# Blocks of 512 tokens in the later MLP parts, and one group for both halves of a query tile

## The chip, the cores and the metric

The kernel runs on one core of a Trainium2 chip. The metric is device time in microseconds (us) of one execution. Five engines work side by side, each through its own queue of instructions in a fixed order: TensorE (PE, matrix products; PEld is its loading of weights), VectorE (DVE), ScalarE (ACT), GpSimd (POOL) and SyncE (SP, which here issues nearly all DMAs).

## The reference

Linear attention with an exponential feature map is followed by two MLPs. There are 4 batches of 576 tokens, 8 heads of 64, 128 features per sign; then 2304 tokens of 512 go through two MLPs with 2048 hidden values each.

```python
def phi(x):
    proj = np.einsum('bhsd,df->bhsf', x, w_phi)
    proj = proj - np.max(np.abs(proj), axis=-1, keepdims=True)
    return np.concatenate([np.exp(proj), np.exp(-proj)], axis=-1)
q_p, k_p = (phi(q), phi(k))
kv = np.einsum('bhsf,bhsd->bhfd', k_p, v)
z = np.sum(k_p, axis=2)
num = np.einsum('bhsf,bhfd->bhsd', q_p, kv)
den = np.einsum('bhsf,bhf->bhs', q_p, z)[..., None] + 1e-06
x = num / den                                    # to (2304, 512)
h = x @ moe_w_in;  g = where(h > 0, h, exp(min(h, 0)) - 1);  x = g @ moe_w_out
h = x @ moe2_w_in; g = h * cos(h);               out = g @ moe2_w_out
```

## The kernel before

`body` builds a list of tasks. A task is a short run of instructions on one engine, with an estimated cost, a due time, the buffers that it writes and reads, and the tasks that it follows. `plan` (called near the end of `body`) then walks a model of the engines: at each step it takes, for the engine that can start first, the ready task with the earliest due time, gives its buffers places out of the lists that they may use, and so fixes the order of every engine. The costs and the due times (`BEGIN`, `BLOCK_A`, `LEAD`, `PACE` and the others at the head of the file) only set this order; on the chip the engines wait for semaphores.

The attention (`shifted`, `keys`, `sums`, `queries`, `results`) goes by tiles of 128 tokens. Heads are split into an even and an odd set of four ("odd" 0 and 1), each with a PSUM bank of its own. For a tile of keys: projection (line 373), maximum of the absolute values and subtraction on DVE (386, 389), two exponentials per set on ACT (423, 426), the product with the values (431) and, for batch 0 only, the sum over keys by a product with ones (437); for the other batches the sums are added up by POOL or DVE and multiplied by ones once (466). For a tile of queries: projection, maximum and subtraction as above, then per set four turns on PE (517), two exponentials (520), 24 small products against the keys' result (535), and the denominator, its reciprocal and the division (543, 546, 549), which write `xy`, the MLP's input.

The MLPs run in three parts: A, the first MLP's hidden tiles 0 to 7 in 9 blocks of 256 tokens (`NA`), between the attention's instructions; B, its hidden tiles 8 to 15; C, the second MLP's 16 hidden tiles. B and C go in 6 blocks of 384 tokens (`NB`) each. In a block, every value of the input is split into a rounded part and a rest (`high`, `low`, 595), and `step` does one hidden tile: `g1`, 12 matmuls into a bank "h" (636: 4 pieces of the input's width, 3 passes each over high and low parts of weight and input), the activation (655, 658, 661 for the first MLP; 670, 673, 676, 679, 682 for the second), its split into high and low (694), and `g2`, 12 matmuls that accumulate into four output banks "y" (644). `AHEAD` sets how many steps `g2` lags. At a block's end four copies and four DMAs take the outputs away (621), or B adds part A's sums from memory (611). Weights come packed and are unpacked on ACT, DVE and POOL (`convert`, 327 to 356).

SBUF places for these pieces are the "units" u0 to u25 (`unit`), of `NB` columns each; the lists `X_U`, `S_A`, `G_A`, `O_A`, `S_B`, `G_B`, `K_B`, `O_B` say which units inputs, split activations, activations and outputs may use. In part C the outputs have three units (17, 24, 25) and the split activations ten.

A change of the shape that the array holds (128 rows by 128 columns in the MLP, 64 by 128 in projections, 128 by 64 and 128 by 32 in the attention's products) is called a switch below.

## Time and profile before

| | us |
|---|---|
| median of 3 runs (1006.4 to 1008.87) | 1006.4 |
| span of the profiled execution, first to last instruction | 1004.8 |
| PE busy in the span | 986.5 |
| DVE busy | 730.0 |
| ACT busy | 496.3 |
| POOL busy | 241.9 |
| first MLP matmul starts at | 52.4 |
| first matmul of 384 columns starts at about | 396 |
| last copy on ACT starts at | 1001.5 |

The table is read from the page, its busy shares and the list of instructions in order of time. PE's busy time counts a matmul from its start to the modelled end of its pipeline, so short waits inside a group don't show in it; the rate of a group is read from the starts of the groups around it.

### The profile page before, as it was taken

How to read it: one execution, taken by the hardware profiler on the slowest of the kernel's cores; microseconds unless marked ns; L12 is line 12 of the kernel's file. 1: busy time of each engine (PE TensorE's matmuls, PEld its weight loads, DVE VectorE, ACT ScalarE, POOL GpSimd, SP SyncE). 2: the span in 40 equal slices, each digit the busy share in tenths (PEclk: the TensorE clock that was granted, in tenths of full speed). 3: DMA queues.
4: the chain of work that ended last, by engine and by line, in shares of the span. 5: the costliest groups of instructions: out<-in, count | busy, mean ns of one | idle time of the engine just before them, and what ended most of it. 6: DMA issues, size and time to landing. Idle time of an engine off the chain costs nothing.

```text
span 1004.8 us, 21194 instructions
## 1 busy us (share of the span) xinstructions
PE 986.5 (98%) x8404; PEld 943.2 (94%) x8404; DVE 730.0 (73%) x1434; ACT 496.3 (49%) x1192; POOL 241.9 (24%) x274
## 2 busy tenths in 40 slices
PE   9999999999999999999999999999999999999998
PEld 6797888998899999999999999999999999999998
DVE  6999788768677986997354699966666666666664
ACT  6987445545545875775232577532332232323322
POOL 2675303103101772774000276400000000000000
PEclk9999999999999999999999999999999999999999
DMA  6463031022102432441012143000000000000000
GB/s 197 163 201 102 7 107 54 30 78 59 39 13 96 151 124 87 160 158 36 8 32 74 64 137 113 29 33 1 1 32 1 1 33 1 33 1 1 32 1 32
DMA packets 46563, 63.30 MB, mean 63 GB/s; under 512 B 6400, under 2 KB 25472, under 8 KB 46464
## 3 DMA queue, kind: packets, MB, share of 16 engines
q1 hardware_dynamic: 46304, 61.88, 18.7%
q8 instruction: 66, 1.08, 0.5%
q14 instruction: 33, 0.27, 0.1%
q10 hardware_dynamic: 160, 0.07, 0.0%
HBM read 52.49 MB, written 9.44 MB: 62 GB/s over the span
## 4 chain that ended last, share of the span: by engine, by line
PE 81%; DVE 8%; POOL 3%; ACT 3%; issue 3%; DMA 1%; DVEq 0%; POOLq 0%; ACTq 0%
PE h L636 21%; PE y L644 20%; PE a L644 13%; PE a L636 13%; PE a L431 4%; PE a L535 4%; PE a L373 3%; POOL l L342 2%; DVE l L338 2%; POOL l L356 2%; PE a L517 1%; DVE l L334 1%; DVE u L694 1%; DVE u L595 1%; ACT l L327 1%
## 5 line engine op out<-in xcount | busy, mean ns | idle before, releaser
L636 PE MATMUL h<-u,h 128*128 128x256 f32 (+1 forms) x1152 | 254.6, 311 | 3.4 <-DVE u L661 3.4
L644 PE MATMUL y<-u,h 128*128 128x256 f32 (+1 forms) x1152 | 254.3, 311 | 1.0 <-DVE u L694 1.0
L636 PEld LDWEIGHTS h<-u,h 128*128 128x128 f32 x1152 | 191.9, 188 | 9.5 <-DVE u L661 4.2
L644 PEld LDWEIGHTS y<-u,h 128*128 128x128 f32 x1152 | 192.3, 188 | 4.6 <-issue 2.3
L644 PE MATMUL y<-u,l 128*128 128x256 f32 (+1 forms) x576 | 177.5, 308 | 0.0
L636 PE MATMUL h<-u,l 128*128 128x256 f32 (+1 forms) x576 | 177.5, 308 | 0.0
L342 POOL TENSOR_TENSOR l<-l,h 128x256 int32<-128x256 int32 x128 | 105.0, 825 | 247.4 <-ACT h L330 102.2
L636 PE MATMUL a<-u,h 128*128 128x384 f32 x576 | 147.3, 337 | 2.0 <-DVE u L595 1.0
L644 PE MATMUL a<-u,h 128*128 128x384 f32 x576 | 146.9, 336 | 0.9 <-DVE u L694 0.9
L694 DVE TENSOR_TENSOR u<-u,u 128x384 fp32r<-128x384 f32 (+1 forms) x216 | 123.1, 570 | 6.1 <-ACT u L240 0.7
L356 POOL TENSOR_TENSOR l<-l,h 128x256 fp32r<-128x256 f32 x128 | 106.7, 843 | 25.2 <-ACT h L353 24.5
L644 PEld LDWEIGHTS y<-u,l 128*128 128x128 f32 x576 | 108.4, 188 | 0.0
L636 PEld LDWEIGHTS h<-u,l 128*128 128x128 f32 x576 | 108.4, 188 | 0.0
L636 PEld LDWEIGHTS a<-u,h 128*128 128x128 f32 x576 | 103.9, 188 | 3.0 <-DVE u L595 1.7
L644 PEld LDWEIGHTS a<-u,h 128*128 128x128 f32 x576 | 104.0, 188 | 1.3 <-DVE u L694 1.3
L679 ACT ACTIVATE u<-u,pihalf 128x384 f32<-128x384 f32 x96 | 59.0, 616 | 90.8 <-DVE u L676 90.7
L636 PE MATMUL a<-u,l 128*128 128x384 f32 x288 | 96.8, 336 | 0.0
L644 PE MATMUL a<-u,l 128*128 128x384 f32 x288 | 96.8, 336 | 0.0
L655 ACT ACTIVATE u<-h 128x256 f32<-128x256 f32 (+1 forms) x96 | 39.1, 407 | 90.4 <-PE h L636 89.0
L242 DVE CAST u<-u 128x384 fp32r<-128x384 f32 (+1 forms) x157 | 61.4, 391 | 29.4 <-PE y L644 19.1
L338 DVE SCALAR_TENSOR_TENSOR l<-raw,l 128x256 uint32<-128x256 uint32 x128 | 72.2, 578 | 0.7
L661 DVE SCALAR_TENSOR_TENSOR u<-u,h 128x256 f32<-128x256 f32 (+1 forms) x96 | 42.6, 445 | 35.3 <-ACT u L658 34.9
(78 smaller groups left out, 1406.5 us busy)
## 6 DMA issues: line engine op xcount, KB each, us to landing
raw<-w SPq DMA_DIRECT2D x128, 256.0 KB, 3.0
qf<-qt SPq DMA_DIRECT2D x18, 256.0 KB, 2.9
part<-u SPq DMA_DIRECT2D x36, 128.0 KB, 1.8
u<-part SPq DMA_DIRECT2D x24, 192.0 KB, 2.5
out<-u SPq DMA_DIRECT2D x24, 192.0 KB, 1.9
kf<-kt SPq DMA_DIRECT2D x16, 256.0 KB, 3.7
vt<-vt SPq DMA_DIRECT2D x16, 256.0 KB, 4.3
kf<-kt SPq DMA_DIRECT2D x4, 128.0 KB, 2.7
```

The costliest lines, as they stand in the source:

```text
L242: engine.tensor_copy(dst, src)
L338: nc.vector.scalar_tensor_tensor(e, raw.tile[:, :, 1], 0x80000000, e, ALU.bitwise_and, ALU.bitwise_or)
L342: nc.gpsimd.tensor_tensor(e, e, r.tile, ALU.add)
L356: nc.gpsimd.tensor_sub(l.tile, f.tile, h.tile.bitcast(F32))
L431: nc.tensor.matmul(kv.tile[at:at + 64, pair * 256:pair * 256 + 256], v.tile[0:r, 2 * i + odd], e.tile[0:r, i].rearrange("p s f -> p (s f)" ...
L535: nc.tensor.matmul(n.tile[32 * h:32 * h + 32, g * P + lo:g * P + hi], k[:, half, h // 2, at:at + 32] if g < 2 else k[:, half, 2, 32 * h:32 ...
L636: nc.tensor.matmul(hp.tile[:, 0:N], columns(W[m, j, 0, kk * P // CH][a], kk), xs[kk][c].tile[:, 0:N], start=(kk == 0 and n == 0), stop=(kk ...
L644: nc.tensor.matmul(yp(dt), columns(W[m, j, 1, dt * P // CH][a], dt), (sh, sl)[c].tile[:, 0:N], start=(i == 0 and n == 0 and (late or dt % ...
L655: nc.scalar.activation(g.tile[:, 0:N], hp.tile[:, 0:N], AF.Relu, scale=-1.0)
L661: nc.vector.scalar_tensor_tensor(g.tile[:, 0:N], g.tile[:, 0:N], -1.0, hp.tile[:, 0:N], ALU.add, ALU.max)
L679: nc.scalar.activation(g.tile[:, 0:N], g.tile[:, 0:N], AF.Sin, bias=pihalf)
L694: nc.vector.tensor_sub(sl.tile[:, 0:N], g.tile[:, 0:N], sh.tile[:, 0:N].bitcast(F32))
```

## The change

`NB` goes from 384 to 512: parts B and C run in four blocks of 512 tokens and one last block of 256. Part A stays at 256. The units have 512 columns; there are 24 of them, and in part A one unit holds a high part and its low part side by side. Seven units come from a new pool "mq" that opens when the attention's pool is released. In part C the split activations have seven units, the outputs four (10, 11, 12, 23). Part A's sums are copied and stored for two output tiles at once.

In the attention both sets of a query tile now share a task: their eight turns are one group on PE and their 48 products another, so the products wait for all four exponentials. The same holds for the product of keys and values with the sums by ones behind it. The planner charges `TURN` where PE goes between MLP groups and others, and prefers by `STICK` to stay with the kind that ran last; its costs and due times have other values.

```diff
-NA, NB = 256, 384
+NA, NB = 256, 512
...
-BEGIN, BLOCK_A, BLOCK_B, BLOCK_C = 30.0, 42.0, 34.0, 68.0
+TURN, STICK = 0.1, 6.45
+BEGIN, BLOCK_A, BLOCK_B, BLOCK_C = 31.56, 42.0, 34.0, 69.09
...
-                c = min((c for c in cand if c[0] <= first), key=lambda c: c[1].due)
+                c = min(
+                    (c for c in cand if c[0] <= first),
+                    key=lambda c: c[1].due - (STICK if e == "PE" and c[1].group == group else 0.0),
+                )
...
+        if engine == "PE":
+            spent += TURN if t.group != group else 0.0
+            group = t.group
...
-    NU = 18
-    X_U = range(8)
-    S_A, G_A, O_A = range(8, 14), (14, 15), (16, 17)
-    S_B, G_B, K_B, O_B = (*range(8, 14), 18, 19, 20, 21), (14, 15, 22), (16, 23), (17, 24, 25)
+    NU, NQ = 13, 7
+    X_A, S_A, G_A, O_A = range(4), range(4, 7), (7, 8), range(9, 13)
+    X_B, S_B = (*range(4), *range(13, 17)), (*range(4, 7), *range(17, 20))
+    S_C, G_C, K_C, O_C = (*S_B, 20), (7, 8, 21), (9, 22), (10, 11, 12, 23)
...
-            for odd in range(2):
-                d, kv, e = ds[odd], kvs[odd], buf("at", "ek", NE, [P, 4, 2, NF])
+            es, done = [buf("at", "ek", NE, [P, 4, 2, NF]) for _ in range(2)], []
+            def times_v(es=es, v=v, t=t, r=r):
+                for odd in range(2):
...
-                if zp:
-                    task("PE", 1.62, du, times_v, [kv, zp], [e, v], [a1, a2])
-                    continue
-                task("PE", 1.06, du, times_v, [kv], [e, v], [a1, a2])
+            task("PE", 2.85 if zp else 1.76, du, times_v, [*kvs, zp] if zp else kvs, [*es, v], done)
...
-        for odd in range(2):
-            results(T, odd, due + odd * pace / 2, parts, ds[odd], done)
+        results(T, due, pace, parts, ds, done)
...
-        task("PE", 0.55, due, turn, [tt], [d, c_id], d.ready)
+        task("PE", 0.87, due, turn, tts, [*ds, c_id], [t for d in ds for t in d.ready])
...
-        task("PE", 1.43 if len(parts) == 1 else 1.9, due, product, [n], [e, *kz], [a1, a2, *done])
+        task("PE", 2.65 if len(parts) == 1 else 3.5, due + pace / 2, product, ns, [*es, *kz], [*acts, *done])
...
-        for dt in range(NK):
-            x, o = cells([dt], c0, N), unit(O_B if m == 2 else O_A)
+        per = 1 if late else 2
+        for d in range(0, NK, per):
+            x, o = cells([d], c0, N), unit(O_C if m == 2 else O_A)
...
-    for c0 in range(0, NT, NB):
-        block(1, 1, c0, NB, due, BLOCK_B)
-        due += BLOCK_B
+    late = [(c0, min(NB, NT - c0)) for c0 in range(0, NT, NB)]
+    for c0, n in late:
+        block(1, 1, c0, n, due, BLOCK_B * n / 384)
+        due += BLOCK_B * n / 384
```

Three places show what this does to the order. The first is PE's queue after the first projections of batch 0's keys (kf, vt and ek are keys, values and exponentials, y is the bank of the sums by ones). Before:

```order
L431 MATMUL a_33_190<-ek_27_165,vt_5_110 64x256 x4
L437 MATMUL y_34_191<-ek_27_165,ones 32x256 x4
L373 MATMUL a_38_213<-ww,kf_23_156 128x128
...
L431 MATMUL a_42_229<-ek_29_169,vt_5_110 64x256 x4
L437 MATMUL y_34_191<-ek_29_169,ones 32x256 x4
```

And in the changed kernel:

```order
L382 MATMUL a_33_191<-ww,kf_23_156 128x128
...
L434 MATMUL a_39_211<-ek_27_165,vt_5_110 64x256 x4
L434 MATMUL a_40_212<-ek_30_172,vt_5_110 64x256 x4
L441 MATMUL y_41_213<-ek_27_165,ones 32x256 x4
L441 MATMUL y_41_213<-ek_30_172,ones 32x256 x4
```

The two sets' products now stand side by side, and then the two sums by ones (of the eight projections between the sets one row is shown).

The second is DVE's queue just ahead of the first MLP block, whose low parts are written from xy into units (l and raw are weights being unpacked). Before:

```order
L549 TENSOR_TENSOR xy<-a_178_754,rd_187_802 128x2x128
L338 SCALAR_TENSOR_TENSOR l_160_665<-raw_159_664,l_160_665 128x256
L334 TENSOR_SCALAR l_165_674<-l_165_674 128x256
L595 TENSOR_TENSOR u_192_819<-xy,u_191_818 128x256
L338 SCALAR_TENSOR_TENSOR l_165_674<-raw_164_673,l_165_674 128x256
L595 TENSOR_TENSOR u_198_843<-xy,u_197_842 128x256
L334 TENSOR_SCALAR l_173_713<-l_173_713 128x256
L595 TENSOR_TENSOR u_200_848<-xy,u_199_847 128x256
L595 TENSOR_TENSOR u_207_886<-xy,u_206_885 128x256
```

And in the changed kernel:

```order
L573 TENSOR_TENSOR xy<-a_177_736,rd_186_807 128x2x128
L251 CAST u_199_847<-xy 128x256
L343 TENSOR_SCALAR l_171_717<-l_171_717 128x256
L631 TENSOR_TENSOR u_199_847<-xy,u_199_847 128x256
L347 SCALAR_TENSOR_TENSOR l_171_717<-raw_170_716,l_171_717 128x256
L343 TENSOR_SCALAR l_181_791<-l_181_791 128x256
L631 TENSOR_TENSOR u_205_872<-xy,u_205_872 128x256
L347 SCALAR_TENSOR_TENSOR l_181_791<-raw_180_790,l_181_791 128x256
L631 TENSOR_TENSOR u_210_932<-xy,u_210_932 128x256
L631 TENSOR_TENSOR u_213_940<-xy,u_213_940 128x256
```

One high part has moved from ACT to DVE, and up to the last low part 19 instructions of line 343 and 19 of line 347 stand, where there were 18 (line 334) and 17 (line 338).

The third is PE's queue at the fifth query tile of the attention (ident is the unit matrix of the turns, kz the keys' result; of an MLP group one row is shown). Before:

```order
L517 MATMUL a_291_1237<-ident,d_195_828 128x128 x4
L644 MATMUL y_235_1018<-u_280_1206,h_1_0_229_986 128x256
...
L517 MATMUL a_303_1283<-ident,d_196_829 128x128 x4
L535 MATMUL a_305_1291<-eq_297_1254,kz_128_534 32x128 x24
L636 MATMUL h_313_1334<-u_191_818,h_0_0_285_1216 128x256
...
L535 MATMUL a_322_1364<-eq_306_1320,kz_151_596 32x128 x24
```

And in the changed kernel:

```order
L531 MATMUL a_267_1177<-ident,d_203_860 128x128 x4
L531 MATMUL a_268_1178<-ident,d_204_861 128x128 x4
L382 MATMUL a_270_1194<-ww,qf_148_597 128x128
...
L697 MATMUL y_239_1047<-u_253_1101,h_1_0_149_607 128x256 x2
...
L697 MATMUL y_239_1047<-u_265_1154,h_1_0_183_795 128x256 x2
...
L554 MATMUL a_295_1277<-eq_274_1206,kz_130_537 32x128 x24
L554 MATMUL a_296_1278<-eq_278_1214,kz_146_586 32x128 x24
```

Where each set went its own way between MLP groups, the eight turns stand together, and after one projection and two MLP groups the 48 products.

## Rows read from the trace of the kernel before

**Rows 1.** The page: the span and the engines' busy time, and the granted clock.
```profile
span 1004.8 us, 21194 instructions
PE 986.5 (98%) x8404; PEld 943.2 (94%) x8404; DVE 730.0 (73%) x1434; ACT 496.3 (49%) x1192; POOL 241.9 (24%) x274
PEclk9999999999999999999999999999999999999999
```
**Rows 2.** Busy time by stretch: length, then each engine's busy time (count), clock, DMA.
```profile
4.00:32.50 28.50, 27.95 (x281) 17.52 (x282) 22.58 (x44) 21.68 (x52) 12.75 (x17) 1.00 0.64 210
32.50:52.40 19.90, 18.93 (x391) 17.09 (x391) 19.82 (x39) 18.61 (x51) 13.09 (x18) 1.00 0.47 159
396.00:1000.55 604.55, 601.62 (x3469) 599.96 (x3467) 412.82 (x805) 251.36 (x567) 107.53 (x128) 1.00 0.13 42
```
**Rows 3.** PE's waits after 57 us: who for whom, total, times, longest.
```profile
PE h L636 <- DVE u L661: 2.7, 3, 1.0
PE a L517 <- DVE d L389: 1.3, 1, 1.3
...
PE a L636 <- DVE u L595: 1.0, 2, 0.9
PE a L636 <- DVE u L682: 1.0, 1, 1.0
PE a L644 <- DVE u L694: 0.9, 1, 0.9
```
**Rows 4.** The chain of waits in parts A and C: start, length, what.
```profile
293.37 2.81 PE h L636 x24
...
300.04 1.62 PE y L644 x12
301.66 2.85 PE h L636 x24
...
653.19 2.08 PE h L636 x12
...
719.75 1.39 PE h L636 x8
```
**Rows 5.** The chain of waits: products of keys, in batch 0 and in batch 1.
```profile
11.78 1.01 PE a L431 x8
12.79 0.57 PE y L437 x8
...
182.80 1.88 PE a L431 x16
184.67 1.00 PE a L466 x16
```
**Rows 6.** DVE by line and shape, 4 to 52.4 us: busy, mean ns, idle before.
```profile
L338 DVE SCALAR_TENSOR_TENSOR l<-raw,l 128x256 uint32<-128x256 uint32 x17 | 8.1, 493 | 0.1
L334 DVE TENSOR_SCALAR l<-l 128x256 uint32<-128x256 uint32 x18 | 7.3, 423 | 0.5 <-ACT l L327 0.5
```
**Rows 7.** Groups by line and shape, whole execution: columns as in rows 6.
```profile
L242 DVE CAST u<-u 128x256 fp32r<-128x256 f32 x47 | 18.7, 399 | 6.0 <-PE y L644 3.7
L673 DVE SCALAR_TENSOR_TENSOR u<-u,h 128x384 f32<-128x384 int32 x48 | 26.5, 551 | 22.2 <-ACT u L670 22.2
L661 DVE SCALAR_TENSOR_TENSOR u<-u,h 128x256 f32<-128x256 f32 x72 | 29.5, 411 | 23.5 <-ACT u L658 23.2
L520 ACT ACTIVATE eq<-a 128x512 f32<-128x512 f32 x72 | 39.3, 601 | 12.2 <-PE a L517 12.2
```
**Rows 8.** Instructions in order of time at the end: start, length, idle before.
```profile
992.32 0.49 ACT L670 ACTIVATE u<-h 128x384 int32<-128x384 f32 x1 [1.83 <-PE h L636]
...
995.73 0.56 DVE L694 TENSOR_TENSOR u<-u,u 128x384 fp32r<-128x384 f32 x1
...
1000.21 0.34 PE L644 MATMUL y<-u,l 128*128 128x384 f32 x1
1001.50 0.48 ACT L240 COPY u<-y 128x384 f32<-128x384 f32 x1 [0.96 <-DMA out<-u]
```

More of the change, by code (lines that the diff above doesn't have):

```diff
@@ L47 @@
 HOP = 0.25
-SLACK = 1.0
+SLACK = 0.97
 HOPS = {
@@ L151, in plan @@
     free.update(START)
-    order, pooled = [], (0.0, 0.0)
+    order, pooled, group = [], (0.0, 0.0), None
     while len(order) < len(tasks):
@@ L176, in plan @@
             held[p] = b
+        if engine == "PE":
+            spent += TURN if t.group != group else 0.0
+            group = t.group
+        if engine == "POOL":
+            pooled = start, start + spent
         t.start, t.end, t.cost = start, start + spent, spent
-        if engine == "POOL":
-            pooled = t.start, t.end
         free[t.engine] = t.end
@@ L418, in keys @@
                 shifted(kf, du, r, ds, (), AP)
+            es, done = [buf("at", "ek", NE, [P, 4, 2, NF]) for _ in range(2)], []
+            def times_v(es=es, v=v, t=t, r=r):
+                for odd in range(2):
+                    for i in range(4):
+                        at, pair = 64 * (i % 2), i // 2
+                        nc.tensor.matmul(
+                            kvs[odd].tile[at:at + 64, pair * 256:pair * 256 + 256],
+                            v.tile[0:r, 2 * i + odd], es[odd].tile[0:r, i].rearrange("p s f -> p (s f)"),
+                            start=(t == 0 and pair == 0), stop=(t == 4), skip_group_check=True,
+                        )
+                for odd in range(2 if zp else 0):
+                    for i in range(4):
+                        nc.tensor.matmul(
+                            zp.tile[32 * i:32 * i + 32, 256 * odd:256 * odd + 256],
+                            ones[0:r], es[odd].tile[0:r, i].rearrange("p s f -> p (s f)"),
+                            start=(t == 0 and odd == 0), stop=(t == 4), skip_group_check=True,
+                        )
             for odd in range(2):
-                d, kv, e = ds[odd], kvs[odd], buf("at", "ek", NE, [P, 4, 2, NF])
+                d, e = ds[odd], es[odd]
                 def exp(d=d, e=e, r=r):
@@ L451, in add @@
                         engine.tensor_add(total.tile[0:r], total.tile[0:r], e.tile[0:r])
-                    task("POOL", sums_of(1024), du, add, [totals[odd]], [e], [a1, a2])
+                    task("POOL", sums_of(1024), du, add, [totals[odd]], [e], two)
                 else:
@@ L599, in block @@
             task("DVE", cost(DVE_, N), due, low, [xl], [xh, *x], port=True)
+            xb.extend([xh, xl] if late else [xh])
         for j in range(j0, j1):
[L601 removed]
+            step(m, j, j - j0, j == j1 - 1, xs, xb, ys, yp, hs, N, due, span / (j1 - j0), late)
         due += span
[L603 to L624 removed]
@@ L626, in step, with rows, staged, fetch @@
-    def step(m, j, i, last, xs, ys, yp, hs, N, due, pace, late):
+        per = 1 if late else 2
+        for d in range(0, NK, per):
+            x, o = cells([d], c0, N), unit(O_C if m == 2 else O_A)
+            def rows(of, d=d):
+                return of[d:d + per, :, c0:c0 + N].rearrange("k p n -> p k n")
+            def staged(o=o):
+                return o.tile[:, 0:per * N].rearrange("p (k n) -> p k n", k=per)
+            if m == 1 and p == 1:
+                def fetch(staged=staged, rows=rows):
+                    nc.sync.dma_start(staged(), rows(part))
+                def add(o=o, d=d):
+                    nc.vector.tensor_add(xy[:, d, c0:c0 + N], yp(d), o.tile[:, 0:N])
+                in_line("o", task("SP", 0.6, due - 15, fetch, [o], cells([d], c0, N, pcell), line["o"], latency=2.2))
+                task("DVE", cost(DVE_, N), due, add, x, [ys[d], o])
+            else:
+                def keep(engine, o=o, d=d):
+                    copy_to(engine, o.tile[:, 0:per * N], ys[d].tile[:, 0:per * N])
+                def store(staged=staged, rows=rows):
+                    nc.sync.dma_start(rows(out if m == 2 else part), staged())
+                in_line("o", task("ACT", copies_of(per * N), due, keep, [o], [ys[d]], line["o"]))
+                task("SP", 0.6, due, store, [] if m == 2 else cells(range(d, d + per), c0, N, pcell), [o], latency=2.0)
@@ L627, in step, with hi, lo @@
+    def step(m, j, i, last, xs, xb, ys, yp, hs, N, due, pace, late):
         wi, wo = ([b for c in range(NC) for b in W[m, j, io, c]] for io in range(2))
         hp = bank(*hs)
-        g = unit(G_A if m == 1 else G_B)
-        sh, sl = unit(S_A if m == 1 else S_B, F32R), unit(S_A if m == 1 else S_B, F32R)
+        G, S = (G_C, S_C) if m == 2 else (G_A, S_B) if late else (G_A, S_A)
+        g, sh = unit(G), unit(S, F32R)
+        sl, at = (unit(S, F32R), 0) if late else (sh, N)
+        def hi():
+            return sh.tile[:, 0:N]
+        def lo():
+            return sl.tile[:, at:at + N]
@@ L666, in step @@
         else:
-            kr = unit(K_B, I32)
+            kr = unit(K_C, I32)
             def turns():
```

193 lines of the change are left out of this document (94 added, 99 removed).

## The prediction

> **What bounds the kernel now.** I read the page first: PE is busy 986.5 of 1004.8 us, at full granted clock throughout, and no other engine comes near [rows 1]. Busy time alone doesn't say how full PE is, so the windows come next. From 4 to 32.5 us PE is busy 27.95 of 28.5 us; from 32.5 to 52.4, where the first MLP matmul starts, DVE is, with 19.82 of 19.90; from 396 to the last matmul at 1000.55, parts B and C, PE is busy 601.6 of 604.55 and DVE only 412.8 [rows 2]. Third, the waits: after 57 us PE's five largest add up to 6.9 us, all for DVE [rows 3]. So, behind the start, time is what PE's instructions take, and a change counts if it makes those fewer or cheaper. Fourth, the chain of waits gives the price of a matmul. In part C it runs from one `g1` at 653.19 to the one 32 groups later at 719.75: 66.56 us for 384 matmuls, 173.3 ns each [rows 4]. At the 2.4 GHz level of the clock 384 columns take 160.0 ns; 13.3 ns are on top. In part A 24 matmuls of 256 columns take 2.81 or 2.85 us, 118 ns each [rows 4], 11.3 over their 106.7.
>
> **Term 1, the later blocks.** Before, B and C have 6 blocks x 24 steps x 24 matmuls = 3456 of 384 columns: 3456 x 0.1733 = 599.0 us. After, 4 x 24 x 24 = 2304 of 512 and 576 of 256. The columns are the same; 576 matmuls fall away, and with them their surcharge. The trace has no matmul of 512 columns of this kind. If the surcharge stays at 13.3 ns, one takes 213.3 + 13.3 = 226.7: 2304 x 0.2267 + 576 x 0.118 = 522.3 + 68.0 = 590.2 us, 8.8 less. Ends: with the 11.3 ns of 256 columns it is 224.6 ns, 13.6 less; with none at all, 213.3 ns, 39.6 less. On the other side, the line through both shapes gives 0.432 ns a column and 228.6 ns, 4.4 less; the full rate of 384 columns, 231.1 ns, gives 1.4 more. I take the constant 13.3, since 384 is the nearest row.
>
> The Trainium skill (TensorE: Matmul & The Clock Gate, Back-to-back issue gap) puts back-to-back matmuls at N/2.4 + 2.5 ns when warm. By it 384 columns would take 162.5 ns, where the rows show 173.3, and 512 would take 215.8; the trace disagrees with it here, and the sum by it would be 25 us lower than mine.
>
> **Term 2, the start.** For batch 0 the two sets' products and sums stand together, and two switches in four go. Before, a key tile costs (1.01 + 0.57) x 2 = 3.16 us; the same two products joined, as batch 1 has them, take 1.88 and a joined sum by ones 1.00, so 2.88 [rows 5]. Five tiles save 1.4 us of the stretch where PE is the bound. Behind it DVE is the bound, and the order puts more ahead of the last low part of the first block: one instruction of line 334 (423 ns) and two of line 338 (493 ns each) [rows 6], and one cast that ACT did (399 ns [rows 7]): 1.8 us. Net +0.4. The ends are -1.4, if DVE has the time in the first stretch (22.58 of 28.5 us busy), and +1.8, if PE's saving is lost.
>
> **Term 3, the end.** At the end four copies follow the last matmuls, and part C has three units for them. The fourth copy idles 0.96 us for the first DMA to free its unit and starts at 1001.50, though the last matmul started by 1000.21 and ended at 1000.55 [rows 2, 8]. With four units it needn't wait: 0.9 less. It also copies 256 columns instead of 384, about 0.1 less by the steps of such instructions (411 against 551 ns in rows 7, less on ACT). Together -1.0; nothing hides it. The ends are 0, if the four DMAs then queue up at the same moment, and -1.2.
>
> **What costs nothing.** The attention's instructions are the same in number. A trip from the MLP to the attention and back costs PE 0.21 us (12 matmuls in 1.62 against half of 2.81 or 2.85 us [rows 4]), but from the first `g1` on the order has 102 switches before and 103 after, so the joined groups bring nothing there: what they save, more frequent trips take back. ACT, DVE, POOL and SP have fewer and longer instructions in B and C (DVE in all 119 rows fewer in the order); that lies beside PE, with 412.8 of 604.55 us busy. If this cover were gone, each would show as a wait of `g2` for its low part. Part A's sums go in 18 DMAs in place of 36 and come back in 20 in place of 24, beside PE. Part C's split activations have 7 units instead of 10. From a bank's first reading to the low part 384 columns take 992.32 to 996.29, 4.0 us [rows 8]; seven instructions grow by about 0.14 us each (the step from 411 to 551 ns for 128 columns [rows 7]), so 5.0 at 512. Three groups of 12 x 0.2267 = 2.7 us stand between the last `g1` and its `g2`: 8.2 us, enough. A pair of units is then needed for about 1.8 steps, and there are three pairs and a half. With 256 columns in the last block the chain is about 3.0, the three groups are 4.2 us. The planner's new numbers move waits about; I leave the 6.9 us as they are, with ends of 0 and twice as much, -6.9 and +6.9.
>
> **Sum.** -8.8 + 0.4 - 1.0 = -9.4. The profiled execution's own 1004.8 becomes 995.4. The median of the runs, 1006.4, lies 1.6 above that span, so I predict 997.0 us.
>
> **Rivals.** *The surcharge grows with the columns.* For it: it is 11.3 at 256 and 13.3 at 384. Against: part A's rows stand among attention work and spread, while 384 is even. On the line, 228.6 ns, the time is 4.4 above mine, 1001.4; at the full rate of 384, 231.1 ns, it is 1007.2, no gain.
>
> *The products wait for four exponentials (the slower side).* Place: part A, every query tile from the third on. A tile's 48 products now wait for four exponentials of 0.60 us [rows 7] and not for two. If PE ran out of MLP work there it would idle 2 x 0.60 = 1.2 us a tile, 16 tiles, 19.2 us: 1016. It decides where less than 4 x 0.60 = 2.4 us of PE work lies between turns and products. Against: in the new order at least one MLP group (1.41 us) lies between them in all tiles from the fourth on and two or more in ten of those 15, mostly with a projection as well. For: ACT also unpacks weights there and runs in order.
>
> *More waits in the new order.* For: unit lists, lags and costs have all changed, and PE's order was fixed from estimates. Twice the waits of rows 3 makes 1004.
>
> *The surcharge vanishes.* At 512 columns, a full bank, nothing would lie over the 213.3 ns: 30.9 less than mine, 966. Both measured shapes speak against it.
>
> **How the numbers follow.** A measurement of this kernel tells a change from none at about 0.3%, 3 us, so faster means below 1003.4. Forecast 0.68, of which 0.66 faster and 0.02 within the bound; growing on the line 0.13 (0.11 and 0.02); at the full rate 0.05 (within); four exponentials 0.07 (slower); more waits 0.05 (within); none on top 0.02 (faster). Faster 0.79, same 0.14, slower 0.07. The range goes from 989 (11.3 ns on top, 4.8 lower, and about 3 us of the waits gone) to 1004 (the line, 4.4 higher, with the start at its upper end, 1.4 more, and a little more waiting); outside lie the full rate, the four exponentials and the vanished surcharge, 0.14, and some of the forecast's own edges.
>
> **What would show it.** In the changed profile: groups of 512 columns in part C 2.72 us apart (term 1; 2.74 is the line, 2.77 the full rate); pairs of keys' products of 1.88 and sums of 1.00 in the first 32 us, and the first MLP matmul within 2 us of 52.4 (term 2); no idle time ahead of the last copy (term 3); PE's waits for DVE between 3 and 10 us, and none of its waits ahead of the query products for exponentials above 0.5 us. I am wrong if part C's groups are 2.77 us or more apart, or if PE idles by more than 10 us between 57 us and the end.

## The result and the profile after

The changed kernel takes 1012.0 us (median of 4 runs, 1010.9 to 1015.2) against 1006.4 of the kernel before: 1.0055 times as long, with a 95% interval from 1.0036 to 1.0073. It is slower. I predicted 997.0 and gave slower 7%. The kernel before, run again beside the experiments in sets of 7 to 24, has medians from 1006.3 to 1008.5, so sets of one and the same kernel differ by up to 2.2 of these 5.6 us.

The page of the changed kernel answers to [rows 1]: the span, the engines' busy time, the granted clock in 40 slices.

```profile
span 1010.7 us, 19909 instructions
PE 992.8 (98%) x7852; PEld 851.8 (84%) x7852; DVE 726.4 (72%) x1315; ACT 484.2 (48%) x1113; POOL 251.5 (25%) x278
PEclk9999999999999999999999999999999999999999
```

PE has 552 matmuls fewer and is busy 6.3 us longer. Busy time by stretch (length, busy time and count of each engine, clock, DMA) answers to [rows 2]; the start now ends at 55.06, the first late matmul stands at 401.30, the last ends at 1007.18.

```profile
4.00:32.50 28.50, 26.68 (x292) 18.57 (x294) 22.49 (x45) 21.42 (x52) 13.18 (x18) 1.00 0.70 220
32.50:55.06 22.56, 20.18 (x404) 18.54 (x403) 21.60 (x42) 19.28 (x52) 14.45 (x20) 1.00 0.54 159
401.30:1007.18 605.88, 604.58 (x2894) 502.19 (x2892) 398.16 (x688) 241.22 (x502) 106.08 (x128) 1.00 0.13 42
```

Cut at the same events, the spans of both profiled executions give this account:

| us | before | after | difference | forecast |
|---|---|---|---|---|
| to the first MLP matmul | 52.4 | 55.1 | +2.7 | +0.4 |
| part A with the attention | 343.5 | 346.2 | +2.8 | 0 |
| late parts B and C | 604.7 | 605.9 | +1.2 | -8.8 |
| behind the last matmul | 4.2 | 3.6 | -0.6 | -1.0 |
| span | 1004.8 | 1010.7 | +6.0 | -9.4 |

PE's waits after 57 us, the five largest (engine, line, who for, total, times, longest), answer to [rows 3].

```profile
PE a L382 <- issue: 2.0, 1, 2.0
PE a L382 <- DVE d L398: 1.8, 2, 1.6
PE a L689 <- DVE u L734: 1.3, 1, 1.3
PE a L554 <- issue: 1.2, 2, 0.8
PE h L689 <- DVE u L713: 1.2, 2, 0.9
```

They add up to 7.5 us, where there were 6.9; in the late parts only 1.3 us are left. So waits didn't eat the late gain. The chain of waits in part C (start, length, what) did not change in kind either, but its pieces are longer than 2.72:

```profile
646.63 2.79 PE a L689 x12
...
652.22 2.76 PE h L689 x12
...
657.78 2.79 PE h L689 x12
```

Groups of 12 stand 2.76 to 2.79 us apart; 2.77 or more I had named as the sign of being wrong. Over all 2302 recorded steps from one 512-column matmul to the next the mean is 232.0 ns, single ones 224 to 238; of the 3446 steps of 384 columns before, 3427 were 173 or 174.

### The profile page after: what moved, and what is told of

The parts are those of the page before. It is cut to its first block, busy times and chain, and to the rows that moved or that the text cites. A ratio compares the mean times of both kernels' runs of the same rounds, so it can differ in the third digit from the quotient of the medians.

```text
span 1010.7 us, 19909 instructions
## 1 busy us (share of the span) xinstructions
PE 992.8 (98%) x7852; PEld 851.8 (84%) x7852; DVE 726.4 (72%) x1315; ACT 484.2 (48%) x1113; POOL 251.5 (25%) x278
## 4 chain that ended last, share of the span: by engine, by line
PE 87%; DVE 8%; ACT 2%; DMA 1%; issue 1%; POOL 1%; DVEq 0%; POOLq 0%; ACTq 0%
PE y L697 24%; PE h L689 23%; PE a L697 14%; PE a L689 14%; PE a L554 4%; PE a L382 3%; PE a L434 2%; PE a L531 1%; DVE m L395 1%; DVE d L398 1%; DMA raw<-w 1%; DVE u L746 1%; DVE l L347 1%; DVE l L343 1%; DVE ek L463 1%
## 5 line engine op out<-in xcount | busy, mean ns | idle before, releaser
L689 PEld LDWEIGHTS h<-u,h 128*128 128x128 f32 x1056 | 176.3, 190 | 24.6 <-issue 3.3
L697 PEld LDWEIGHTS y<-u,h 128*128 128x128 f32 x1056 | 175.2, 188 | 21.6 <-issue 2.7
L689 PE MATMUL a<-u,h 128*128 128x512 f32 (+1 forms) x480 | 137.7, 372 | 1.3 <-DVE u L734 1.3
L697 PE MATMUL a<-u,h 128*128 128x512 f32 (+1 forms) x480 | 138.3, 372 | 0.0
L746 DVE TENSOR_TENSOR u<-u,u 128x256 fp32r<-128x256 f32 (+1 forms) x192 | 126.9, 661 | 14.4 <-PE y L697 5.0
L697 PEld LDWEIGHTS y<-u,l 128*128 128x128 f32 x528 | 99.4, 188 | 8.6
L689 PEld LDWEIGHTS a<-u,h 128*128 128x128 f32 x480 | 86.8, 188 | 18.9 <-DVE u L734 1.7
L731 ACT ACTIVATE u<-u,pihalf 128x512 f32<-128x512 f32 (+1 forms) x80 | 54.4, 680 | 96.5 <-DVE u L728 96.2
L697 PEld LDWEIGHTS a<-u,h 128*128 128x128 f32 x480 | 86.7, 188 | 16.3
L689 PE MATMUL a<-u,l 128*128 128x512 f32 (+1 forms) x240 | 89.2, 372 | 0.0
L697 PE MATMUL a<-u,l 128*128 128x512 f32 (+1 forms) x240 | 89.2, 372 | 0.0
L251 DVE CAST u<-u 128x256 fp32r<-128x256 f32 (+1 forms) x137 | 58.6, 428 | 23.3 <-PE y L697 14.7
L463 POOL TENSOR_TENSOR ek<-ek,ek 128x1024 f32<-128x1024 f32 (+1 forms) x16 | 41.3, 2590 | 128.4 <-ACT ek L454 123.0
```

Of the source, the lines that this page charges most:

```text
L251: engine.tensor_copy(dst, src)
L463: engine.tensor_add(total.tile[0:r], total.tile[0:r], e.tile[0:r])
L689: nc.tensor.matmul(hp.tile[:, 0:N], columns(W[m, j, 0, kk * P // CH][a], kk), xs[kk][c](), start=(kk == 0 and n == 0), stop=(kk == NK - 1 ...
L697: nc.tensor.matmul(yp(dt), columns(W[m, j, 1, dt * P // CH][a], dt), (hi, lo)[c](), start=(i == 0 and n == 0 and (late or dt % 2 == 0)), s ...
L731: nc.scalar.activation(g.tile[:, 0:N], g.tile[:, 0:N], AF.Sin, bias=pihalf)
L746: nc.vector.tensor_sub(lo(), g.tile[:, 0:N], hi().bitcast(F32))
```

## Experiments

Three things are to be explained: the 512-column step, part A's 2.8 us and the start's 2.7. My first theory of the step was that it is 226.7 by itself and that DVE and ACT beside it lengthen it.

### The step by itself

e1 is a stream of matmuls of the same kind (float32r, three passes of 12) with no other engine at work; only the width changes.

```python
for n, at in SETS:       # 256, 288, ... 512 columns; then 512 and 384 shifted by 64 columns
    for g in range(14):  # 12 matmuls into one of two banks
        nc.tensor.matmul(b[:, 0:n], ws[w][:, k * P:k * P + P], xs[2 * x + k % 2][:, at:at + n], ...)
```

> Only matmuls of the MLP's kind (float32r, weights reloaded each time, pattern of three passes), 14 groups of 12 per width, no other engine at work; it computes nothing of the reference. Theory A, the time goes with the columns (0.4514 ns each, as 384 columns have it): 256 takes 116 to 118 ns, 320 takes 144.4, 416 takes 187.8, 448 takes 202.2, 480 takes 216.7, 512 takes 231 to 232. Theory B, 13.3 ns on top of the columns up to a size, and 512 alone is slow: 416 takes 186.7, 448 takes 200.0, 480 takes 213.3, 512 takes 232. Theory C, the 232 ns comes from the surroundings in the kernel (VectorE and ScalarE at work, where the pieces lie): 512 takes 226.7 here, and shifted by 64 columns something else.

Measured: 256 columns 119.95 ns, 384 173.35, 416 188.3, 448 206.7, 480 216.7, 512 226.7 to 226.9; shifted by 64 columns 226.7 and 173.5. The constant surcharge of 13.3 ns holds here to 0.3 ns at 256, 384 and 512 columns (not between: 15.0 at 416, 20.0 at 448, 16.7 at 480), so something in the kernel adds 5.2 at 512.

e7 puts DVE or ACT beside the stream, reading SBUF or PSUM.

```python
for i in range(34):  # beside groups 2 to about 9 of the 12
    nc.vector.tensor_sub(a0[:, 0:384], src[:, 0:384], a1[:, 0:384])   # or nc.scalar.activation(...)
```

> Matmul streams alone on PE, 12 groups of 12 at 512 and at 384 columns, each with nothing beside, then with DVE reading SBUF, DVE reading PSUM, ACT reading SBUF, ACT reading PSUM beside its first half; it computes nothing of the reference. Theory C: 512 columns step 226.8 with nothing beside and 231 to 238 beside at least one kind; 384 columns step 173.3 whatever is beside. If only the PSUM readers lengthen the step, it is PSUM that is shared; if only one engine does, it is that engine's traffic. Theory D (only the order of the matmuls matters): 226.8 in all five at 512 columns.

Windows of e7 (length, then PE, PEld, DVE, ACT, POOL busy and count): 512 columns alone, beside DVE on SBUF, beside ACT on PSUM.

```profile
21.50:53.50 32.00, 32.00 (x143) 26.50 (x142) 0.00 (x0) 0.00 (x0) 0.00 (x0) 1.00 0.00 1
54.20:70.00 15.80, 15.80 (x71) 13.09 (x70) 12.32 (x23) 0.00 (x0) 0.00 (x0) 1.00 0.00 0
157.00:173.00 16.00, 16.00 (x72) 13.24 (x72) 0.00 (x0) 14.74 (x30) 0.00 (x0) 1.00 0.01 2
```

And 32 us of part C in the changed kernel:

```profile
700.00:732.00 32.00, 32.00 (x139) 25.79 (x139) 19.08 (x31) 8.93 (x15) 0.00 (x0) 1.00 0.09 34
```

A count takes in the matmuls cut at both edges, some 1.5. 143 in 32 us is the step of 226.7, 139 that of 232.0. By single steps e7 has 226.66 or 226.67 while DVE or ACT reads SBUF or PSUM, no step above 227. The theory falls: beside this stream neighbours do nothing.

Next I saw in the kernel's steps that a run of 226 and 227 breaks off at the first one or two matmuls of a group, where PE waits for others' results. e8 gives each group a wait for something long ready, or a signal.

```python
xs = fresh[...]              # one operand per 12, 24 or 48 matmuls, each written by DVE long before
nc.tensor.matmul(b[:, 0:n], ws[w][:, k * P:k * P + P], xs[g][:, 0:n], ...)
if kind == "signal":
    nc.vector.tensor_copy(xs[g], raw[:, g % 4])
```

> Matmul streams alone on PE, 144 matmuls each, DVE's work long done or only reading after; it computes nothing of the reference. Theory E (a wait on PE's own queue shifts the hand-over from one 512-column matmul to the next, and it takes about nine matmuls to fall back to 226.7): 512 columns with a wait (for something long ready) every 12 matmuls step 231 to 233 on the mean, every 24 about 229, every 48 about 228; without waits, and with a signal but no wait, 226.7; 384 columns with a wait every 12 step 173.3. Rival (it is what the other engines do, not PE's waits): 226.7 in all five 512-column streams.

Measured: 226.66 or 226.67 in all five, with twelve waits or none; 384 columns 173.5. This theory falls as well.

Then I set the places of the operands in SBUF beside the steps. In the four kernels with blocks of 512 run by then, three steps of 226 or 227 in a row were followed by a longer one in 253 of 929 cases (the text of e11 below has 574 for the 929): always where the moving operand came from above 198 kB of the partition, never from below. e12 moves that operand through the partition and at the end the stationary one.

```python
AT = {"a": 40960, "b": 122880, ..., "h": 204800, "i": 221184}   # places of the moving operand
SETS = [(512, x, x, "w") for x in "abcdefghi"] + [(512, "a", "h", "w"), (512, "a", "a", "z"), ...]
```

> Matmul streams alone on PE, 96 matmuls each, no other engine at work; it computes nothing of the reference. At 512 columns the moving operand stands at nine places between 41 and 221 kB of the partition, then alternates between 41 and 205 kB, then the stationary operand goes to 213 kB; then 384 columns at 205 and 41 kB. Theory A: 226.7 ns at 41 to 188 kB and 231 to 236 from 198.7 kB up; 173.3 at 384 at either place; a high stationary operand alone does nothing. Rival: 226.7 at every place, the address matters only together with what the kernel does beside.

Windows of e12: moving operand at 41 kB and at 205 kB, then at both places with the weights moved to 213 kB.

```profile
23.50:44.50 21.00, 21.00 (x92) 17.05 (x91) 0.00 (x0) 0.00 (x0) 1.00 0.00 1
180.00:201.00 21.00, 21.00 (x92) 17.00 (x92) 0.00 (x0) 0.00 (x0) 1.00 0.00 0
246.60:267.60 21.00, 21.00 (x94) 17.40 (x93) 0.00 (x0) 0.00 (x0) 1.00 0.00 1
268.30:289.30 21.00, 21.00 (x94) 17.40 (x93) 0.00 (x0) 0.00 (x0) 1.00 0.00 0
```

232.3 to 232.5 ns at all nine places, 226.67 with the other weights: the height of the address is not it, and the expected 226.7 below 188 kB was wrong. What the streams share is a difference. In bytes modulo 256, e12's moving operands start 128 past the first weights and 0 past the second; in e1, e7 and e8 it is 0; in the changed kernel it is 0 for half of the 512-column matmuls (units in the new pool) and 160 for the others. I call it the shift. e15 changes nothing else.

```python
SETS = [(n, 8 * s) for n in (512, 384, 256) for s in range(8)] + [(512, 64)]   # start in columns of 4 bytes
nc.tensor.matmul(banks[g % 2][:, 0:n], ws[i][:, k * P:k * P + P], x[:, at:at + n], ...)
```

> Matmul streams alone on PE, 96 matmuls each; it computes nothing of the reference. At 512, 384 and 256 columns the moving operand starts 0, 32, ... 224 bytes past the place of the stationary one, modulo 256 bytes, then 512 columns at a shift of 256 bytes. Theory M (the step depends on where the moving operand starts against the stationary one, modulo 256 bytes: in the kernel 160 and in the run before 128 give 232 to 234 at 512 columns, 0 gives 226.7): 512 columns 226.7 at 0 and at 256, 231 to 236 at 128 and 160; 384 columns 173.3 at 0 and 160, 176.0 at 128; 256 columns 120 at 0 and 118.2 at 160. Rival (it is the place of the stationary operand by itself): the same step at every shift of a width.

Mean step in ns over the second half of each stream:

| shift in bytes | 0 | 32 | 64 | 96 | 128 | 160 | 192 | 224 | 256 |
|---|---|---|---|---|---|---|---|---|---|
| 512 columns | 226.7 | 233.3 | 228.9 | 233.3 | 233.3 | 234.3 | 233.3 | 233.3 | 226.7 |
| 384 columns | 173.3 | 173.3 | 173.3 | 176.7 | 175.9 | 173.3 | 174.7 | 173.3 | |
| 256 columns | 120.0 | 117.8 | 117.8 | 120.0 | 118.8 | 117.4 | 113.3 | 118.3 | |

Windows of e15: 512 columns at shifts 0 and 160 (21 us), 256 columns at 0 and 192 (10.5 us).

```profile
21.40:42.40 21.00, 21.00 (x94) 17.38 (x94) 0.00 (x0) 0.00 (x0) 1.00 0.00 1
132.90:153.90 21.00, 21.00 (x91) 16.91 (x90) 0.00 (x0) 0.00 (x0) 1.00 0.00 1
334.00:344.50 10.50, 10.50 (x90) 10.50 (x90) 0.00 (x0) 0.00 (x0) 1.00 0.01 2
401.70:412.20 10.50, 10.50 (x95) 10.50 (x95) 0.00 (x0) 0.00 (x0) 1.00 0.01 2
```

At shift 160 the 512-column steps go round 232, 237, 238, 231, 234, 235, 233, the series that the changed kernel shows. In a stream that keeps to one shift, the shift sets the step, and each width has good shifts of its own. All streams of e7 and e8 are at shift 0; whether neighbours or waits matter at another shift they don't show.

### The shift in the kernels

e11 is the changed kernel with every engine's instructions in the same order; only pools change places. Nearly all moving operands of the MLP get shift 0.

```diff
-    cst, xp, dr = pool("cst"), pool("xp"), pool("dr", space=DRAM)
+    cst, xp, dr = pool("cst"), pool("xp", side="right"), pool("dr", space=DRAM)
+    pool("mp")
     pool("wa")
...
-    pool("mp", side="right")
```

> The changed kernel with every engine's instructions in the same order, only the places in SBUF changed: the pool with most of the MLP's moving operands at the bottom (2880 to 29504 bytes of a partition), the attention's result at the top (192480 to 229344). Theory A (address: of 574 locked steps in the traces of the four kernels with blocks of 512, 253 were lost, each where the moving operand came from above 198 kB, and none elsewhere): the 512-column matmul steps 226.7 to 227.5 in place of 232.0, 2304 x 5 ns = 11 us off the late parts, which take 594 to 595; span 998 to 1001, ratio 0.992 to 0.995. Rival (it is the order of the groups, whatever the address): 232.0 again, span 1008 to 1013.

1004.5 us, ratio 0.997 (0.9952 to 0.9988) to the kernel before. The late parts take 595.9 us, 10.0 less than in the changed kernel; the groups stand 2.72 us apart:

```profile
646.36 2.72 PE a L689 x12
649.08 1.36 PE a L697 x6
650.44 1.36 PE y L697 x6
651.80 2.72 PE h L689 x12
```

It was written for the theory of the address. That theory had all of these units below 198 kB and so locked; but one unit at 188 kB with shift 160 steps 232.0 there, while the others step 227.1. The span came to 1004.5, above the 998 to 1001 expected, because part A lost 3.7 us (349.9): its 256-column step went from 118.2 to 119.7, near the 120.0 of shift 0 alone, which makes 2.6 us for 1728 steps, and PE idles 1.1 us more there. Steps by shift in the profiled executions (count; small groups left out):

| kernel | 256 columns | 384 columns | 512 columns |
|---|---|---|---|
| before | 160: 118.2 (1632) | 160: 173.3 (3447) | |
| after | 160: 118.2 (1887) | | 0: 230.4 (1127); 160: 233.6 (1175) |
| e11 | 0: 119.7 (2146) | | 0: 227.1 (2190); 160: 232.0 (112) |
| e16 | 192: 115.2 (1976) | | 0: 227.3 (1472); 192: 233.1 (716) |
| e17 | 192: 115.3 (1627) | 0: 173.5 (2066); 192: 175.7 (956); 96: 176.7 (192); 160: 176.8 (227) | |
| e2 | 160: 118.0 (1598) | 0: 174.5 (1681); 160: 176.1 (1752) | |
| e10 | 160: 118.0 (1623) | 160: 174.1 (3446) | |

In the changed kernel even shift 0 has 230.4: behind a stretch at 160 it takes up to nine steps to come back to 226.7.

The shift is not all. At 384 columns 160 is a good shift alone and in the kernel before, but e2, e10 and e17 have 174 to 177 ns there. In e10 (below), whose operands lie as in the kernel before, the 384-column steps are 174 and 179 in turn, 176.7 on the mean, from 465 to 614 us, and 173.3 ahead of it and behind it. Both ends stand at an idle time of PE. Windows of e10, in the stretch and behind it:

```profile
470.00:502.00 32.00, 32.00 (x183) 32.00 (x182) 15.87 (x35) 9.69 (x20) 0.00 (x0) 1.00 0.09 26
700.00:732.00 32.00, 32.00 (x186) 32.00 (x185) 20.81 (x43) 9.37 (x18) 0.00 (x0) 1.00 0.01 2
```

So what ran just before counts too; which of the two patterns a stretch falls into, and why, no run settles.

### Part A and the start

e2, e3, e5 and e6 each keep a part of the change. e2 is the changed kernel with blocks of 384 (its units keep 512 columns):

```diff
-NA, NB = 256, 512
+NA, NB = 256, 384
```

> The changed kernel with blocks of 384 tokens in the later parts again, all else as changed. If the width's price is what the later parts lost: 3456 x 0.1733 = 599.0 us of matmuls in place of 2304 x 0.232 + 576 x 0.118 = 602.5, so 3.5 us less than the changed kernel, 1008.5 us, the start and part A as slow as in the changed kernel. If 512 columns cost what I had forecast and the loss is in the order alone: 1012 or, since the numbers were set for 512, more (1020).

1025.1 us, ratio 1.0169 (1.0147 to 1.0192), late parts 615.9: with the new numbers and places 384 is worse than 512. That is 11.2 us over the kernel before, of which the longer steps (175.3 ns on the mean, with the shift going between 0 and 160) make 6.8. e3 is the changed kernel with the planner's old numbers:

```diff
-BEGIN, BLOCK_A, BLOCK_B, BLOCK_C = 31.56, 42.0, 34.0, 69.09
+BEGIN, BLOCK_A, BLOCK_B, BLOCK_C = 30.0, 42.0, 34.0, 68.0
...
-NL, W1LATE, NEQ, EARLY = 5, -18.28, 4, 177.85
+NL, W1LATE, NEQ, EARLY = 5, -20.0, 4, 180.0
```

> The changed kernel (blocks of 512, joined groups, TURN and STICK) with the planner's due times and leads of before (BEGIN to EARLY; five spare places for low parts and four for exponentials stay, since the memory doesn't hold more). If the new numbers cause the waits between 55 and 125 us: those 5.5 us of start and part A come back, 1006.5 us. If the joined groups cause them: no less than 1011 us, with PE's waits ahead of projections as in the changed kernel.

1012.7 us, ratio 1.0049 (1.0023 to 1.0074): part A 3.0 us shorter, the late parts 2.6 longer, the start as late. So the new numbers cost part A its loss and give nearly as much back in the late parts; the start isn't theirs, and as a whole they are not the cause. e5 has the MLP's side alone (blocks, units, their costs), e6 the attention's alone, each on the kernel before with its numbers:

```diff
-NA, NB = 256, 384
+NA, NB = 256, 512
...
+TURN, STICK = 0.0, 0.0
```

> Only the MLP side of the change: late blocks of 512 with their units, the attention's tasks and the planner's numbers as in the kernel before. Theory C (neighbours: a 512-column matmul takes 226.8 ns alone and 232.0 beside DVE and ACT): start 52.4 and part A 343.5 as before, late parts 601.8 + 2.8 + some 3 of waits = 607.5, tail 3.6, so a span of 1007 and a ratio of 1.002. Theory D (the 232 ns comes from the new order, with its joined groups): 512 columns at 226.8, late parts 593 to 596, span 993 to 996, ratio 0.99. If the start is 55 here too, the packed halves of the early blocks' inputs make it late, and not the joined groups.

```diff
-                task("PE", 1.06, du, times_v, [kv], [e, v], [a1, a2])
+            task("PE", 2.85 if zp else 1.76, du, times_v, [*kvs, zp] if zp else kvs, [*es, v], done)
...
-            results(T, odd, due + odd * pace / 2, parts, ds[odd], done)
+        results(T, due, pace, parts, ds, done)
```

> Only the attention side of the change: one PE task for a tile's kv and z products and one for a query tile's turns and products; blocks of 384 and all numbers as before. Theory J (a joined product waits for the slower of two halves): first MLP matmul at 55.0 instead of 52.4, part A longer by 0 to 3, late parts as before, span 1007.5 to 1010, ratio 1.003 to 1.005. Rival (the joined groups are free and the loss lies in the units and the numbers): start 52.4, span within 0.7 of 1004.8, ratio 1.000.

e5: 1014.7 us, ratio 1.0077 (1.0052 to 1.0102). Its first MLP matmul stands at 52.7 and its late parts take 607.6, as expected with 232.0; but part A takes 349.3, which wasn't: PE has 46 more matmuls in it, one 3.4 us piece at the 1.2 GHz level, and idles 2.3 us more than before. e6: 1015.3 us, ratio 1.0093 (1.0062 to 1.0123), first MLP matmul at 58.8, part A 340.6, late parts 609.8. So the joined groups make the start late and part A 2.9 us shorter; why, and why 58.8 where e3 with four places for a query tile's exponentials has 55.1 and e6 has three, isn't shown. The late parts' 5.1 us more than before, with the same blocks, are longer 384-column steps as in e10 (456 to 612 us, 2.9 us in all) and waits.

Part A loses most in one place of the changed kernel, 80 to 118 us. Windows there, before and after:

```profile
80.00:118.00 38.00, 36.72 (x342) 30.05 (x340) 33.60 (x65) 24.80 (x60) 19.18 (x16) 1.00 0.20 64
```

```profile
80.00:118.00 38.00, 34.07 (x284) 27.44 (x282) 37.69 (x56) 23.43 (x54) 23.67 (x18) 0.91 0.31 91
```

DVE is busy throughout with fewer instructions, PE idles, and its clock falls. DVE's rows in order of time (start, length), then POOL's:

```profile
89.53 0.41 DVE L746 TENSOR_TENSOR u<-u,u 128x256 fp32r<-128x256 f32 x1
89.87 2.49 DVE L251 CAST u<-xy 128x256 fp32r<-128x256 f32 x1
...
104.47 2.60 DVE L746 TENSOR_TENSOR u<-u,u 128x256 fp32r<-128x256 f32 x1
107.00 2.60 DVE L347 SCALAR_TENSOR_TENSOR l<-raw,l 128x256 uint32<-128x256 uint32 x1
```

```profile
89.67 2.54 POOL L463 TENSOR_TENSOR ek<-ek,ek 128x1024 f32<-128x1024 f32 x1 [2.27 <-ACT ek L454]
...
104.36 4.96 POOL L463 TENSOR_TENSOR ek<-ek,ek 128x1024 f32<-128x1024 f32 x2
```

The same subtraction takes 0.41 us and then 2.60: while POOL adds up keys, these DVE instructions stand. From 57 to 140 us stretching beside those sums adds 9.9 us to DVE in the changed kernel, 2.5 before. The Trainium skill (SBUF — State Buffer, Who interferes with whom) says that DVE, in some of its instructions, and GpSimd share a port pair that one holds for a whole instruction while the other stands; these rows agree. The planner knows this for some tasks (`port`), but its sums now fall beside DVE's. PE idles 1.95 us ahead of 95.39 (the profile names no releaser; one of DVE's subtractions of line 398 has just ended), and the clock drops:

```profile
94.00:97.00 3.00, 1.43 (x12) 1.29 (x14) 3.00 (x9) 1.63 (x3) 0.37 (x1) 0.87 0.69 208
97.00:100.00 3.00, 3.00 (x19) 2.77 (x17) 3.00 (x3) 0.98 (x3) 3.00 (x2) 0.57 0.00 0
```

Two pieces of 3.4 us run at the 1.2 GHz level, the second from 113.3, behind PE's idle time at 109.9. They match part A's loss: from the first MLP matmul to the first late one PE is busy 3.4 us longer than before, with as many matmuls, and idles 0.7 us less (windows before, then after).

```profile
52.38:395.87 343.49, 335.83 (x4262) 306.78 (x4259) 274.39 (x544) 202.75 (x522) 107.86 (x106) 1.00 0.25 80
```

```profile
55.06:401.33 346.27, 339.27 (x4264) 310.74 (x4261) 283.44 (x537) 201.06 (x508) 117.16 (x110) 0.99 0.26 78
```

e9 takes the sums from POOL.

```diff
     def sums_of(n):
-        return {"POOL": cost(POOL_, n), "DVE": cost(DVE_, n)}
+        return {"DVE": cost(DVE_, n)}
```

> The changed kernel with the key sums that POOL may take given to DVE alone, so that no 2.5 us sum of POOL stands beside DVE. Theory P (POOL's sums hold DVE up: 9.9 us of stretched DVE work at 57 to 140 us, and PE idles behind it at 93 and 110 us and drops to half clock twice): the five sums cost DVE 5 x 1.21 = 6.1 us there, 9.9 us of stretching go, the two PE idles of 2.3 and 1.9 us go and with them most of the two half-clock pieces; part A falls from 346.3 to 341 to 344, span 1005 to 1008. Rival (DVE is simply overloaded there, whoever adds): part A 346 to 350, span 1010 to 1014.

1010.9 us, ratio 1.0019 (0.9994 to 1.0043); its runs overlap with the changed kernel's. No DVE instruction stands through a sum any more (the shorter work of POOL still lengthens some by up to 0.6 us), and in part A the clock stays at full speed: PE is busy 2.9 us less there. But it idles 1.6 us more, and part A is 344.9, only 1.3 less; a sum costs DVE up to 1.75 us and not 1.21. The mechanism is there, its price smaller than I expected. With the low places (e13 against e11) the same edit takes 4.7 us off part A.

### The fourth output, and better kernels

e4 is the kernel before with one more output unit in part C; e10 adds the sums on DVE to it.

```diff
-    S_B, G_B, K_B, O_B = (*range(8, 14), 18, 19, 20, 21), (14, 15, 22), (16, 23), (17, 24, 25)
+    S_B, G_B, K_B, O_B = (*range(8, 14), 18, 19, 20, 21), (14, 15, 22), (16, 23), (17, 24, 25, 26)
```

> The kernel before with a fourth unit for part C's outputs and nothing else. If the last copy's wait for a unit is a cost of its own: 0.9 us less, 1005.5 us, and no idle time ahead of the last copy. If the four DMAs at the end only queue up: the same 1006.4 us.

> The kernel before with a fourth output unit and its key sums on DVE alone: a version that may beat both. Theory P: DVE is stretched by only 2.5 us at 57 to 140 us in the kernel before, and PE waits there 3.5 us in two places, so the gain is at most 2 us; with 0.9 us from the fourth unit, span 1001 to 1004, ratio 0.997 to 0.999. Rival: the sums that DVE takes over (4 x 1.22 us) make it late for PE, span 1004 to 1008, ratio 1.000 to 1.004.

e4's time can't be told from before (1.0001, 0.9973 to 1.0028), but its profile ends 3.3 us behind the last matmul, not 4.2. e10: 1.0008 (0.9974 to 1.0041), part A 1.8 us longer, late parts 2.5, for which its 384-column steps (above) suffice; the order before hardly had the collision, so there was little to win.

e13 has e11's places and e9's sums; e14 the same on e5 (with the attention's own groups); e16 chooses the shift by width, and starts the last block's operands 48 columns in; e17 moves the pools of the kernel before in the same way.

> The places of the run before with the key sums on DVE alone: the changed kernel with both of its losses taken away that the runs found. Theories A and P together: start 54.7, part A 345, late parts 594 to 595, tail 3.6, span 997 to 999, ratio 0.990 to 0.993. Rival (the attention's result at the top slows what reads it): part A 348 or more.

> Blocks of 512 with the low places and the sums on DVE, the attention's tasks and all numbers as in the kernel before. Theory J as well (the joined groups make the start late): start 52.5, part A 344 to 347, late parts 594 to 597, tail 3.6, span 995 to 999, ratio 0.988 to 0.992. Rival (the joined groups do the work of part A good): part A 349 as with the width alone, span 999 to 1002.

```diff
-    cst, xp, dr = pool("cst"), pool("xp"), pool("dr", space=DRAM)
     pool("wa")
+    cst, xp, dr = pool("cst"), pool("xp", side="right"), pool("dr", space=DRAM)
+    pool("mp")
...
-    pool("mp", side="right")
```

> The kernel of the run with low places and the sums on DVE, its pools set so that part A's 256-column operands start 192 bytes past their weights modulo 256 (113.3 ns alone, against 120 at 0) and the 512-column ones 0 past them, but 192 past those of the second layer's first eight pieces, which share part A's place. Theory M: part A loses 1728 x (119.7 - 113.5) = 10.7 us, a third of the 512-column matmuls go from 227.4 to 233.3 (768 x 6 = 4.6 us more), the last block of 256 saves some 2; span 1000.9 - 8 = 993, ratio 0.985 to 0.988. Rival (part A is bound by DVE and ACT when PE's steps get shorter): part A stays at 342 or more, span 999 to 1002.

> The kernel before, the same instructions in the same order on every engine, its pools set so that part A's 256-column operands start 192 bytes past their weights modulo 256 in place of 160. Theory M: 1728 x (118.2 - 113.5) = 8.1 us less in part A; at 384 columns most stay at 173.3, 960 at a shift of 192 pay 1.4 ns and 192 at a shift of 96 pay 3.3, 1.9 us more; span 1004.8 - 6 = 998.5, ratio 0.992 to 0.995. Rival (only 512 columns care, 256 do not in the kernel): span 1003 to 1006, ratio 1.000.

| | us | ratio to before (95%) | start | part A | late parts |
|---|---|---|---|---|---|
| e13 | 1002.7 | 0.9936 (0.9913 to 0.9959) | 55.1 | 345.3 | 597.0 |
| e14 | 1009.7 | 1.0014 (0.9998 to 1.0030) | 52.7 | 353.5 | 598.5 |
| e16 | 1000.1 | 0.9932 (0.9918 to 0.9947) | 54.5 | 340.4 | 599.6 |
| e17 | 1007.7 | 0.9997 (0.9977 to 1.0017) | 52.5 | 340.8 | 609.2 |

e13 and e16 are faster than the kernel before by 0.6 to 0.7%, and so than the changed one; they can't be told apart. In e16 twelve 256-column matmuls take 1.36 us where the changed kernel has 1.42 (chain of waits in part A, e16 and after):

```profile
150.84 1.36 PE h L690 x12
152.20 1.36 PE y L698 x12
```

```profile
158.02 1.43 PE y L697 x12
159.45 1.42 PE h L689 x12
```

That saved 4.9 us of part A, not 10.7, and the span is 998.1, not 993: in the kernel the step comes to 115.2 and not to the 113.5 of the sum, which is 3.0 us over 1728 steps, and PE idles 1.7 us more, as the rival had it in kind; 1.1 is not placed. e17 won 2.7 us of part A, not 8.1: its step came to 115.3, and PE idles 1.4 us more. Its late parts gave 4.5 us back, more than the 1.9 expected; besides shifts 96 and 192 the pieces at 160 lost too. So it is no faster. e14 fell short: its start is 2.4 us earlier than e13's, as expected, and its part A 8.3 longer. It differs from e13 in the joined groups and in the planner's numbers, so it doesn't tell which; that the joined groups help part A rests on e6.

## Why the prediction was wrong

**Term 1 failed, in its size.** It took the 13.3 ns over the full rate from 384 columns and put 512 at 226.7. The blocks and counts were right, and so was the mechanism, fewer surcharges: alone, at shift 0, a step takes 226.7. In the changed kernel it took 232.0, for 2304 matmuls 12.2 us more than the term had, and the 8.8 us became a loss of 3.4; 1.6 us less waiting in the late parts and 0.6 that is not placed leave the measured 1.2. The row I took for the nearest, 384 columns, was measured at shift 160, where in that kernel 384 pays nothing extra, and where 512 alone pays 7.7 ns; no row of before could show that. e15 shows the shift alone; e11 gives the late parts 10.0 us back by places alone.

The rival at 231.1 ns came nearest in size, but its reason, a surcharge that grows with the columns, isn't what the runs show. By the formula of the Trainium skill (TensorE: Matmul & The Clock Gate, Back-to-back issue gap), which the page gives for an isolated matmul, a 512-column step would be 215.8 ns, an estimate; no stream of 512 columns here has a mean below 226.7.

**Term 2 failed.** The joined products came as priced (1.88 and 1.00 us, in the chain of the changed kernel, answering to [rows 5]):

```profile
13.05 1.88 PE a L434 x16
14.93 1.00 PE y L441 x16
```

But the first stands 1.3 us later than before, behind the next projection (11.80, 1.25 us), which PE's new order puts ahead of it; the four exponentials had ended at 11.78. PE's saving did arrive: batch 0's last sum by ones ends at 31.28 and not at 32.52 (chain of waits, before and after):

```profile
31.91 0.61 PE y L437 x8
```

```profile
30.28 1.00 PE y L441 x16
```

It brought the first MLP matmul nothing, because DVE is the bound there. From 4 us on DVE is busy 44.1 us up to it, 1.7 more than before, nearly the 1.8 priced, and it idles 7.0 us, 1.0 more; together these are the 2.7. The sum took PE's 1.4 off the start where it could at best have shortened DVE's idle time, and that grew: DVE waits 1.6 us for a projection that stands behind the eight joined turns, and longer for ACT (DVE's waits up to the first MLP matmul, before and after):

```profile
DVE m L386 <- PE a L373: 7.5, 2, 5.5
DVE l L334 <- ACT l L327: 0.5, 1, 0.5
DVE m L386 <- PE h L373: 0.4, 1, 0.4
```

```profile
DVE m L395 <- PE a L382: 6.3, 2, 5.4
DVE m L395 <- PE h L382: 1.8, 2, 1.6
DVE l L343 <- ACT l L336: 1.7, 2, 0.9
```

e5 (no joined groups, 52.7) and e6 (only these, 58.8) place the delay with the joined groups. There too it is DVE's work ahead of the first MLP matmul that counts: 42.4 us before, 42.6 in e5, 47.1 in e3, 49.6 in e6.

**"The planner's new numbers move waits about; I leave the 6.9 us" failed for part A.** The sum of the waits held (7.5). What I put at nothing is the clock behind two of them, 3.4 us, and DVE's standing beside POOL; with the old numbers (e3) part A is 3.0 us shorter. The order shows where POOL's sums stand; I had left it out.

**Term 3 held.** The last copies wait for no DMA, and the end is 0.6 us shorter than before, 1.0 forecast (rows in order of time, answering to [rows 8]):

```profile
1006.15 0.78 DVE L251 COPY u<-a 128x256 f32<-128x256 f32 x2 [1.23 <-PE a L697]
1006.86 0.78 DVE L251 COPY u<-y 128x256 f32<-128x256 f32 x2
```

**What costs nothing held in the late parts**: part C's seven units for split activations are enough, with 1.3 us of waits. The rival of the four exponentials in part A didn't come: no wait for them stands in the list. It had given the slower side its 7%, so that side came for other reasons.

## What to carry to other kernels

The price of a matmul's shape holds for the places its operands had: before pricing a new width, measure it at the shift that the allocation will give it, or choose the shift. When a scheduler's numbers change, look not only at PE's order but at what POOL now runs beside DVE. A saving on one engine shortens a stretch only if that engine is the bound there: for the start, count the other engine's work and waits ahead of its end.

## What the runs showed of the hardware

The step between float32r matmuls with a weight load each depends on where the moving operand starts past the stationary one, modulo 256 bytes: in streams of one shift 226.7 to 234.3 ns at 512 columns, 173.3 to 176.7 at 384, 113.3 to 120.0 at 256. The best shift differs by width (0 for 512, 192 for 256). The height of the address changes nothing (e12); at shift 0, neither do DVE and ACT beside or waits long satisfied (e7, e8). The shift alone doesn't settle it: at 384 columns and shift 160, e10 has 173.3 ns in most of its late parts and 176.7 for 150 us between two idle times of PE. Why this is so the runs don't show. At the best shifts a column costs the same at 256 and 512 columns, 0.443 ns.
